# Query and key weights of two kinds of attention layer: kept on chip, or loaded block by block

## The chip, the cores and the metric

The kernel runs on one core of one Trainium2 chip. The metric is the device time of one execution in microseconds (us). The kernel before was run three times for its time, and once more with the hardware profiler, from which come the trace and the profile page.

## The reference

Four attention layers are applied in turn to an input of 2048 rows and 640 columns in bf16, each as `x = x + attention(layernorm(x))`. There are 32 heads of 20 columns. Layers 0 and 2 (kind A) let a row see itself and the 255 rows ahead of it; layers 1 and 3 (kind B) let each row see all rows. Layers of one kind share their weights.

```python
def _A_ref(x, wqkv, wo):
    B, S, D = x.shape
    H = 32; Dh = D // H; W = 256
    qkv = (lambda x, *d: x.transpose(*d))((x @ wqkv).reshape(B, S, 3, H, Dh), 2, 0, 3, 1, 4)
    q, k, v = qkv[0], qkv[1], qkv[2]
    scores = jnp.einsum("bhqd,bhkd->bhqk", q, k) * (Dh ** -0.5)
    idx = jnp.arange(S)
    mask = (idx[:, None] - idx[None, :] >= 0) & (idx[:, None] - idx[None, :] < W)
    scores = jnp.where(mask[None, None], scores, -1e9)
    p = _softmax(scores, axis=-1)
    o = jnp.einsum("bhqk,bhkd->bhqd", p, v)
    return (lambda x, *d: x.transpose(*d))(o, 0, 2, 1, 3).reshape(B, S, D) @ wo
...
x = x + _A_ref(_layernorm(x, axis=-1), A_wqkv, A_wo)
x = x + _B_ref(_layernorm(x, axis=-1), B_wqkv, B_wo)
x = x + _A_ref(_layernorm(x, axis=-1), A_wqkv, A_wo)
x = x + _B_ref(_layernorm(x, axis=-1), B_wqkv, B_wo)
```

`_B_ref` is the same without the mask. The layer norm has no scale and no offset.

## The kernel before, in words

**Stages and tiles.** The rows are cut into 4 chunks of 512 (`C`). For each layer and chunk the kernel normalises the rows and transposes them into a tile `xnT` of 128 x 5 x 512 (`t_ln`, L410), projects queries, keys and values from it, forms the attention, and adds the product with the output weights to `x_sb`, which stays on chip (`t_out`, L565). Heads go in 8 groups of four, one head to each 32 rows or columns of the PE array. A unit (`Unit`, L694) is one layer, chunk and group, for layers 1 and 3 also a part of the keys. All units stand in one list (L752 to L768), in which windowed units of layer A are woven between full ones of layer B.

**The main loop** (L1371) writes the program tile by tile. For each tile t it takes two or three score blocks of the current unit, has PE form them in PSUM (L1416), and ACT take the exponentials into a tile `pt` (L1442). Two or three tiles later PE multiplies `pt` by the values (L1475). For windowed units GpSimd (POOL in the profile) sets the masked part of `pt` to zero with selects (L1515), and VectorE (DVE) multiplies by mask tiles (L1526).

**Background work.** All else is a list of generators, `todo` and `tails`, sorted by the unit that needs them, of which `pump` (L265) advances some between two tiles by a credit. `require` (L299) is the way out: when a unit begins and something it needs is missing, tasks are advanced with no tiles in between. Each engine works its instructions in the order written; Tile adds the semaphores. `keep_clock` (L671) and `unread` (L659) add idle matmuls of `masks` by `ident` where PE has little to do.

**Query and key weights before.** In the first chunk of layer 0 (`t_qk_first`, L530) each group's 80 columns are copied from `raw`, which holds the weights of kind A, into a padded tile with 20 of every 32 columns used (`get_w`, L355 to L362: a memset on GpSimd and a copy on DVE, 16 times). Everywhere else (`t_block`, L545) a task projects 128 dense columns, one of 5 blocks of the queries or keys, and stores the result to DRAM (L554, on GpSimd's queue). For each of these 15 x 10 = 150 tasks `get_w` loads the block of weights from DRAM on GpSimd's queue (L353, 160 KB) into one of 8 buffers of the pool `wqkp`. `take_w` (L364) starts the loads of up to two blocks ahead, and holds the task until four tiles after its load was issued (`wtick`).

**Other queues.** SP's queue (SyncE) first loads the input and the weights of the start (L128 to L138), then the output weights (L150), and, as they come due, each unit's queries, keys and values (`load_unit`, L781). GpSimd's queue also carries the stores of projections and values and, in `t_ln`, the square root of each chunk's norm (L421, L424).

**Normed rows.** The pool `xtp` has five `xnT` buffers; `room` (L320) lets a task go on only while fewer than `cap` are in use, and `used` (L329) gives one back when all its 9 to 12 projections are written.

**DVE's share of the exponentials.** In layers 1 and 3 a part of the score blocks goes in pairs to DVE, which forms the exponential by arithmetic (`side_fixed`, L975, `chain`, L997). `side_start` (L911) sets up its scratch tiles for layer 3 from three `xnT` buffers that are no longer in use; `side_early` (L924) does so for layer 1 in another tile.

Of the kernel before, what the change touches and what calls it, by code (L numbers as in the profile page):

```python
# [9 lines left out]
BF16 = mybir.dt.bfloat16  # L10
# [8 lines left out]
P = 128  # L19
S = 2048  # L20
D = 640
# [38 lines left out]
def kernel(  # L60
# [14 lines left out]
    def pool(name, bufs, space=None):  # L75
        kw = {"space": space} if space else {}
        return ctx.enter_context(tc.tile_pool(name=name, bufs=bufs, **kw))

    big = pool("big", 1)
    wqkp = pool("wqkp", 8)  # L80
    kvp = pool("kvp", 3)
    vap = pool("vap", 10)
    xtp = pool("xtp", 5)
    onp = pool("onp", 2)
    ptp = pool("ptp", 6)
    stp = pool("stp", 4)
# [12 lines left out]


    x_sb = big.tile([P, NT, D], BF16, name="x_sb", tag="x_sb")
    raw = big.tile([P, KD, 2 * D], BF16, name="raw", tag="early_late")
    wv_sb = [big.tile([P, KD, D], BF16, name=f"wv{w}", tag=f"wv{w}") for w in range(2)]
    wop = big.tile([P, G, D], BF16, name="wop", tag="wop")
    ident = big.tile([P, P], BF16, name="ident", tag="ident")
# [209 lines left out]
            nc.tensor.matmul(out_[r], lhsT=lhsT[:, r], rhs=rhs, start=start, stop=stop)  # L315

    live = Counter()
    cap = {"qa": QA, "ka": KA, "va": 10, "xnT": 5, "kt": 3, "vt": 3, "qt": 4, "ln": 1, "w": 4, "vs": 2}

    def room(*tags):  # L320
        while any(live[t] + tags.count(t) > cap[t] for t in tags):
# [4 lines left out]

    users = {}

    def used(l, c):  # L329
        users[l, c] -= 1  # L330
        if users[l, c] == 0:
            live["xnT"] -= 1

    def evac(out_, in_):
        if state["act"]:
# [4 lines left out]


    wtiles = {}
    worder = {(l, n): [] for l in range(4) for n in range(2)}

    wtick = {}

    def get_w(l, n, c, i):

        t = wqkp.tile([P, KD, P], BF16, name="wqk", tag="wqk")
        wtick[l, n, c, i] = state["tick"] + 4  # L350
        if l or c:
            a = n * D + i * P
            nc.gpsimd.dma_start(out=t[:], in_=wq_view[l % 2][:, :, a : a + P])  # L353
            return t
        tv = t[:].rearrange("p c (j m) -> p c j m", j=4)  # L355
# [5 lines left out]
        wtick[l, n, c, i] = 0  # L361
        return t  # L362

    def take_w(l, n, c, i):  # L364
        key, order = (l, n, c, i), worder[l, n]
        if key not in wtiles:
            wtiles[key] = get_w(*key)
        while state["tick"] < wtick[key]:
            yield ("wait", 1)
        at = order.index(key)  # L370
        order.pop(at)
        wt = wtiles.pop(key)
        for e in order[at : at + 2]:
            if e not in wtiles and sum(o in wtiles for o in order) < 2 and len(wtiles) < 4:
                wtiles[e] = get_w(*e)
        return wt

    staging = []

# [30 lines left out]
    def t_ln(l, c):  # L410
        while ("x", l, c) not in ready:
            yield ("wait", 1)
        yield from room("xnT", "ln")
        for n in (1, 0):
            order = worder[l, n]
            if order and not any(e in wtiles for e in order):
                wtiles[order[0]] = get_w(*order[0])
# [12 lines left out]
        xt = xtp.tile([P, KD, C], BF16, name="xnT", tag="xnT")  # L430

        def normed(i):
            state["lag"] += 0.5
            xn = xnp.tile([P, D], BF16, name="xn", tag="xn")
            nc.vector.tensor_scalar(
                out=xn[:], in0=x_sb[:, 4 * c + i, :],
                scalar1=rstd[:, i : i + 1], scalar2=nmr[:, i : i + 1],
                op0=ALU.mult, op1=ALU.add,
            )
# [24 lines left out]
        ready.add(("xnT", l, c))  # L464
# [65 lines left out]
    def t_qk_first(l, c, g):  # L530
        while ("xnT", l, c) not in ready:
            yield ("wait", 1)
        yield from room("qa", "ka", "w", "w")
        wt = yield from take_w(l, 0, c, g)
        q = qa_free.popleft()
        yield from project(wt, xnT[l, c], lambda: q[:])
        wt = yield from take_w(l, 1, c, g)
        k = ka_free.popleft()
        yield from project(wt, xnT[l, c], lambda: k[:])
        live["w"] -= 2  # L540
        qa[c, g], ka[c, g] = q, k
        used(l, c)
        ready.add(("qk", l, c, g))

    def t_block(l, n, c, b):  # L545

        while ("xnT", l, c) not in ready:
            yield ("wait", 1)
        yield from room("w")
        wt = yield from take_w(l, n, c, b)  # L550
        yield from project(wt, xnT[l, c], staged)
        rows = slice(b * P, (b + 1) * P)
        dst = k_d[l][rows, c * C : (c + 1) * C] if n else q_d[l][c, rows, :]
        nc.gpsimd.dma_start(out=dst, in_=staging.pop())  # L554
        live["w"] -= 1
        used(l, c)
        ready.add(("qk"[n], l, c, b))

# [67 lines left out]
    def push_layer(l, c):  # L626
# [10 lines left out]
        if c or l:  # L637
            for b in range(KD):
                g = b * P // 80
                for n in (1, 0):  # L640
                    worder[l, n].append((l, n, c, b))
                    first = index[l, c, g, PARTS[l][0] if l % 2 and c == 0 else None]
                    first = need[g] if n else first
                    push(("qk"[n], l, c, b), t_block(l, n, c, b), first, 1.1)
            return
        for g in range(G):
            for n in (0, 1):
                worder[l, n].append((l, n, c, g))
# [261 lines left out]

    def side_start():  # L911

        assert live["xnT"] <= 2 and not side["chain"] and side["half"] is None
        tl = [xtp.tile([P, KD, C], BF16, name="xnT", tag="xnT") for _ in range(3)]
        live["xnT"] += 3
        f = [v[:, 0:4, :].rearrange("p a b -> p (a b)").bitcast(F32) for v in tl]
        side["xi"].clear()
        side["out"].clear()
        outs = [ka_all[:, KA - 6 + 2 * n : KA - 4 + 2 * n, :] for n in range(3)]
        outs += [qa_all[:, 2 * n : 2 * n + 2, :] for n in range(2)]  # L920
        side_tiles(f[0:2], f[2].bitcast(F16)[:, 0 : 2 * C], outs)
        side["late"] = True

    def side_early():  # L924
# [311 lines left out]
    def first_ln():  # L1236

        users[0, 0] = 9
        live["xnT"] += 1
        xt = xtp.tile([P, KD, C], BF16, name="xnT", tag="xnT")  # L1240

        def warm(count):
            for n in range(count):
# [42 lines left out]
        warm(3)  # L1286
        nc.vector.tensor_copy(out=xt[:, :, P : 2 * P], in_=trs[1])
        for n in (1, 0):
            wtiles[0, n, 0, 0] = get_w(0, n, 0, 0)
# [6 lines left out]
    with tc.manual_schedule():  # L1296
# [74 lines left out]
        while ended is None or t < ended + 8:  # L1371
# [3 lines left out]
            if flow:  # L1375
                if not side["early"] and state["unit"] >= index[1, 1, 0, None]:
                    side_early()
                if (
                    not side["late"] and state["unit"] >= index[3, 0, 4, PARTS[3][0]]
                    and live["xnT"] <= 1 and not live["qa"] and not live["ka"]  # L1380
                ):
                    side_start()
                if state["unit"] >= final:
# [191 lines left out]
```

## Time and profile before

| | us |
|---|---|
| three runs: median (lowest, highest) | 2168.42 (2165.64, 2171.8) |
| the profiled execution, its own time | 2167.19 |
| span of its trace | 2165.5 |
| ACT busy in it | 2086.1 |
| PE busy | 1924.8 |
| DVE busy | 1488.7 |
| POOL busy | 485.9 |

The span is the time from the first to the last instruction on the core, and lies 1.7 us below that execution's own time. A busy engine is one that executes; its waits are listed as idle time, with what ended them. PEld is PE's loading of weights, which lies beside its matmuls. Traffic with DRAM is 99.52 MB read and 27.79 MB written.

### The profile page before, as it was taken

The page shows a single profiled execution, that of the slowest core. Times are in us where ns is not written, and L with a number is a line of the kernel's source. Part 1 is how long each engine was busy: PE and PEld are TensorE (multiplying, and loading weights), DVE is VectorE, ACT ScalarE, POOL GpSimd, SP SyncE. Part 2 cuts the span into 40 slices and gives each one's busy share as a digit, 9 for nine tenths or more (in the row PEclk, how much of TensorE's full clock was granted, in tenths as well). Part 3 has the DMA queues.
Part 4 walks back from the last instruction along what each step waited for, and adds up shares of the span by engine and source line. Part 5 has one row for each costly group of instructions (what it writes and reads, how often), then busy time and mean ns, then how long its engine had stood idle before and what let it go on. Part 6 is the DMA issues. An engine that isn't in the chain of part 4 may idle for free. (4 is left out here: it accounts for less than half of the span.)

```text
span 2165.5 us, 73279 instructions
## 1 busy us (share of the span) xinstructions
PE 1924.8 (89%) x31759; PEld 754.6 (35%) x31759; DVE 1488.7 (69%) x2625; ACT 2086.1 (96%) x1717; POOL 485.9 (22%) x953
## 2 busy tenths in 40 slices
PE   8999999988889898888988989888898898888898
PEld 4444443433333333333333433332332222222222
DVE  5656665426666776776767733676779887888896
ACT  7889899999999999999999999989999999999997
POOL 6665546110122113410053112511000000000000
PEclk9999999999999999999999999999999999999999
DMA  6223233322211323112241133112121111111100
GB/s 204 76 84 107 75 92 101 81 80 64 79 45 27 84 61 90 41 41 61 56 112 33 37 86 99 39 42 77 53 60 44 35 36 42 32 33 39 42 30 17
DMA packets 88418, 137.29 MB, mean 63 GB/s; under 512 B 20766, under 2 KB 63486, under 8 KB 88094
## 3 DMA queue, kind: packets, MB, share of 16 engines
q1 hardware_dynamic: 68878, 79.43, 13.9%
q0 software_dynamic: 19216, 53.17, 8.3%
q8 instruction: 249, 4.08, 0.8%
q14 instruction: 75, 0.61, 0.1%
HBM read 99.52 MB, written 27.79 MB: 59 GB/s over the span
## 5 line engine op out<-in xcount | busy, mean ns | idle before, releaser
L1442 ACT ACTIVATE pt<-ps 128x1536 bf16<-128x1536 f32 (+2 forms) x1641 | 2051.7, 1406 | 46.4 <-PE ps L1416 35.5
L1416 PE MATMUL ps<-qt,kt 32*128 32x512 bf16 x3914 | 544.6, 383 | 59.8 <-ACT pt L1442 52.5
L315 PE MATMUL ps<-masks,ident 128*32 128x512 bf16 x5652 | 505.6, 384 | 96.6 <-ACT pt L1442 47.5
L1475 PE MATMUL ps<-pt,vt 128*21 128x512 bf16 x3774 | 375.9, 386 | 1.8 <-issue 1.0
L1416 PEld LDWEIGHTS <-kt 32*128 32x128 bf16 x3914 | 154.7, 91 | 460.2 <-issue 440.4
L315 PEld LDWEIGHTS <-ident 128*32 128x32 bf16 x5652 | 180.3, 94 | 278.9 <-issue 253.5
L1515 POOL TENSOR_SCALAR_AFFINE_SELECT pt<-pt 128x256 bf16<-128x256 bf16 (+2 forms) x506 | 217.1, 451 | 187.6 <-ACT pt L1442 175.3
L315 PE MATMUL ps<-xnT,wqk 128*32 128x512 bf16 x3320 | 225.2, 381 | 11.9 <-DMA wqk<-in_B_wqkv_dram 2.1
L339 DVE CAST st<-ps 128x512 bf16<-128x512 f32 x134 | 92.5, 690 | 143.9 <-PE ps L315 143.6
L1475 PEld LDWEIGHTS <-vt 128*21 128x21 bf16 x3774 | 93.4, 89 | 260.1 <-issue 256.3
L989 DVE TENSOR_SCALAR xnT<-ps 128x512 int32<-128x512 f32 x210 | 144.1, 687 | 34.6 <-PE ps L971 27.5
L315 PE MATMUL ps<-wop,on 128*32 128x320 bf16 x3712 | 160.5, 300 | 5.7 <-DVE x_sb L587 3.9
L1526 DVE TENSOR_TENSOR pt<-pt,masks 128x256 bf16<-128x256 bf16 (+3 forms) x268 | 113.4, 438 | 46.5 <-ACT pt L1442 44.3
L315 PEld LDWEIGHTS <-on 128*32 128x32 bf16 x5760 | 122.3, 95 | 63.7 <-issue 29.8
L1416 PE MATMUL ps<-qa,ka 32*128 32x384 bf16 (+2 forms) x1408 | 118.0, 276 | 22.5 <-ACT pt L1442 19.1
L587 DVE TENSOR_TENSOR x_sb<-x_sb,ps 128x320 bf16<-128x320 bf16 x120 | 58.2, 485 | 101.6 <-PE ps L315 101.1
L1185 DVE TENSOR_TENSOR on<-on,ps 128x512 bf16<-128x512 bf16 x128 | 86.4, 684 | 59.2 <-PE ps L315 57.0
L315 PE MATMUL ps<-wv,xnT 128*32 128x320 bf16 x2560 | 116.0, 301 | 9.0 <-DVE vs L339 2.0
L315 PEld LDWEIGHTS <-wqk 128*32 128x32 bf16 x3320 | 83.2, 96 | 96.0 <-issue 38.1
L989 DVE TENSOR_SCALAR raw_o<-ps 128x512 int32<-128x512 f32 x112 | 76.8, 686 | 47.3 <-PE ps L1416 46.8
L890 DVE CAST on<-ps 128x512 bf16<-128x512 f32 x112 | 76.7, 685 | 37.9 <-PE ps L1475 30.7
L554 POOL DMA_DIRECT2D k_d<-st x75 | 42.5, 567 | 225.7 <-DVE st L339 213.0
(99 smaller groups left out, 1797.9 us busy)
## 6 DMA issues: line engine op xcount, KB each, us to landing
vt<-v_d SPq DMA_DIRECT2D x48, 336.0 KB
kt<-k_d SPq DMA_DIRECT2D x192, 80.0 KB
wqk<-in_B_wqkv_dram POOLq DMA_DIRECT2D x80, 160.0 KB, 3.5
wqk<-in_A_wqkv_dram POOLq DMA_DIRECT2D x70, 160.0 KB, 3.6
k_d<-st POOLq DMA_DIRECT2D x75, 128.0 KB, 2.5
q_d<-st POOLq DMA_DIRECT2D x75, 128.0 KB, 2.3
qt<-q_d SPq DMA_DIRECT2D x384, 20.0 KB
v_d<-vs POOLq DMA_DIRECT2D x16, 336.0 KB, 3.0
```

The lines of the kernel that those rows point to most:

```text
L315: nc.tensor.matmul(out_[r], lhsT=lhsT[:, r], rhs=rhs, start=start, stop=stop)
L339: nc.vector.tensor_copy(out=out_, in_=in_)
L554: nc.gpsimd.dma_start(out=dst, in_=staging.pop())
L587: nc.vector.tensor_tensor(out=xv, in0=had, in1=yp, op=ALU.add)
L890: nc.vector.tensor_copy(out=oT, in_=op)
L989: nc.vector.tensor_scalar(out=xi.bitcast(I32)[:, i * C : (i + 1) * C], in0=z, scalar1=SCALE * LOG2E * FIX, scalar2=127.5 * FIX, op0=ALU.mu ...
L1185: nc.vector.tensor_tensor(out=oT, in0=oT, in1=zb, op=ALU.mult)
L1416: nc.tensor.matmul(sp[:, i, col * P : (col + qn) * P], lhsT=u.k(kc, j), rhs=u.q(j, q0, qn), start=True, stop=True,)
L1442: nc.scalar.activation(out=pt[:, i:k, b0 * P :], in_=sp[:, i:k, b0 * P :], func=ACT.Exp, scale=SCALE,)
L1475: nc.tensor.matmul(op[32 * j : 32 * j + VW, q0 * P : (q0 + qn) * P], lhsT=u.v(kc, j), rhs=pg[:, i, col * P : (col + qn) * P], start=(first ...
L1515: nc.gpsimd.affine_select(out=v, in_=v, compare_op=ALU.is_gt if later else ALU.is_ge, fill=0.0, base=0, pattern=[[0, k - i], [-1 if later ...
L1526: nc.vector.tensor_tensor(out=pt_[:, i:k, cols], in0=pt_[:, i:k, cols], in1=mv_, op=ALU.mult)
```

## The change

- The pools `wqkp` and `xtp` go. One tile `xt_all` has two slots for normed rows in the place of five buffers, handed out by `take_xt` and given back by `used`.
- One tile `spare`, as large as three of the former buffers, holds `raw` (kind A's query and key weights) and behind it the last 256 columns of kind B's. A tile `wqk` of 1024 columns is first the eight padded buffers of the first chunk and then holds the first 1024 columns of kind B's.
- After the last padded projection two loads on SP's queue bring kind B's weights. Tasks of layers 1 and 3 are not started before these loads are written.
- `t_block` takes its weights from these tiles (`block_w`). There are no loads by block, no order of loads and no holding for four tiles; `t_ln` starts no load.
- `side_start` takes its scratch from `spare`, over `raw`, at a point where layer 2's projections are all written, and no longer looks at how many `xnT` buffers are in use.

```diff
-    wqkp = pool("wqkp", 8)
-    xtp = pool("xtp", 5)
...
-    raw = big.tile([P, KD, 2 * D], BF16, name="raw", tag="early_late")
+    xt_all = big.tile([P, 2, KD, C], BF16, name="xnT", tag="xnT")
+    spare = big.tile([P, 3 * KD * C], BF16, name="spare", tag="spare")
+    raw = spare[:, 0 : KD * 2 * D].rearrange("p (c f) -> p c f", c=KD)
+    wqk_rest = spare[:, KD * 2 * D :].rearrange("p (c f) -> p c f", c=KD)
+    wqk = big.tile([P, KD, 8 * P], BF16, name="wqk", tag="wqk")
...
-    cap = {"qa": QA, "ka": KA, "va": 10, "xnT": 5, "kt": 3, "vt": 3, "qt": 4, "ln": 1, "w": 4, "vs": 2}
+    cap = {"qa": QA, "ka": KA, "va": 10, "xnT": 2, "kt": 3, "vt": 3, "qt": 4, "ln": 1, "w": 4, "vs": 2}
...
-        wtick[l, n, c, i] = state["tick"] + 4
-        if l or c:
-            a = n * D + i * P
-            nc.gpsimd.dma_start(out=t[:], in_=wq_view[l % 2][:, :, a : a + P])
-            return t
...
-        while state["tick"] < wtick[key]:
-            yield ("wait", 1)
...
+    def block_w(l, n, b):
+
+        a = n * D + b * P
+        if l % 2 == 0:
+            return raw[:, :, a : a + P]
+        if a < 8 * P:
+            return wqk[:, :, a : a + P]
+        return wqk_rest[:, :, a - 8 * P : a - 7 * P]
...
+        if g == G - 1:
+            nc.sync.dma_start(out=wqk[:], in_=wq_view[1][:, :, 0 : 8 * P])
+            nc.sync.dma_start(out=wqk_rest, in_=wq_view[1][:, :, 8 * P : 2 * D])
+            ready.add("weights")
...
-        yield from room("w")
-        wt = yield from take_w(l, n, c, b)
+        while l % 2 and "weights" not in ready:
+            yield ("wait", 1)
+        wt = block_w(l, n, b)
...
-        tl = [xtp.tile([P, KD, C], BF16, name="xnT", tag="xnT") for _ in range(3)]
-        live["xnT"] += 3
-        f = [v[:, 0:4, :].rearrange("p a b -> p (a b)").bitcast(F32) for v in tl]
+        f = [spare[:, n * 4 * C : (n + 1) * 4 * C].bitcast(F32) for n in range(2)]
...
-                    and live["xnT"] <= 1 and not live["qa"] and not live["ka"]
+                    and not live["qa"] and not live["ka"]
```

More of the change, by code (lines that the diff above doesn't have):

```diff
@@ L327, with take_xt @@
     users = {}
+    xt_free = deque(range(2))
+    xt_n = {}
+    def take_xt(l, c):
+        xt_n[l, c] = xt_free.popleft()
+        return xt_all[:, xt_n[l, c]]
     def used(l, c):
@@ L332, in used @@
             live["xnT"] -= 1
+            xt_free.append(xt_n.pop((l, c)))
     def evac(out_, in_):
@@ L342, with get_w @@
     wtiles = {}
[L343 to L349, printed above, removed]
-        wtick[l, n, c, i] = state["tick"] + 4
-        if l or c:
-            a = n * D + i * P
-            nc.gpsimd.dma_start(out=t[:], in_=wq_view[l % 2][:, :, a : a + P])
-            return t
-        tv = t[:].rearrange("p c (j m) -> p c j m", j=4)
+    worder = {(0, n): [] for n in range(2)}
+    padded = [0]
+    def get_w(n, i):
+        a = padded[0] % 8 * P
+        padded[0] += 1
+        t = wqk[:, :, a : a + P]
+        tv = t.rearrange("p c (j m) -> p c j m", j=4)
         nc.gpsimd.memset(tv[:, :, :, DH:32], 0.0)
@@ L360, in get_w, with take_w @@
         )
-        wtick[l, n, c, i] = 0
         return t
-    def take_w(l, n, c, i):
-        key, order = (l, n, c, i), worder[l, n]
+    def take_w(n, i):
+        key, order = (n, i), worder[0, n]
         if key not in wtiles:
             wtiles[key] = get_w(*key)
-        while state["tick"] < wtick[key]:
-            yield ("wait", 1)
         at = order.index(key)
@@ L413, in t_ln @@
         yield from room("xnT", "ln")
[L414 to L417, printed above, removed]
         users[l, c] = 9 if (l, c) == (0, 0) else (11, 12, 11, 11)[l]
@@ L429, in t_ln @@
         )
-        xt = xtp.tile([P, KD, C], BF16, name="xnT", tag="xnT")
+        xt = take_xt(l, c)
         def normed(i):
@@ L533, in t_qk_first @@
         yield from room("qa", "ka", "w", "w")
-        wt = yield from take_w(l, 0, c, g)
+        wt = take_w(0, g)
         q = qa_free.popleft()
         yield from project(wt, xnT[l, c], lambda: q[:])
-        wt = yield from take_w(l, 1, c, g)
+        wt = take_w(1, g)
         k = ka_free.popleft()
@@ L554, in t_block @@
         nc.gpsimd.dma_start(out=dst, in_=staging.pop())
-        live["w"] -= 1
         used(l, c)
@@ L640, in push_layer @@
                 for n in (1, 0):
-                    worder[l, n].append((l, n, c, b))
                     first = index[l, c, g, PARTS[l][0] if l % 2 and c == 0 else None]
@@ L647, in push_layer @@
             for n in (0, 1):
-                worder[l, n].append((l, n, c, g))
+                worder[l, n].append((n, g))
             push(("qk", l, c, g), t_qk_first(l, c, g), need[g], 2.2)
@@ L911, in side_start @@
     def side_start():
-        assert live["xnT"] <= 2 and not side["chain"] and side["half"] is None
-        tl = [xtp.tile([P, KD, C], BF16, name="xnT", tag="xnT") for _ in range(3)]
-        live["xnT"] += 3
-        f = [v[:, 0:4, :].rearrange("p a b -> p (a b)").bitcast(F32) for v in tl]
+        assert not side["chain"] and side["half"] is None
+        assert ("k", 2, NC - 1, KD - 1) in ready and ("q", 2, NC - 1, KD - 1) in ready
+        f = [spare[:, n * 4 * C : (n + 1) * 4 * C].bitcast(F32) for n in range(2)]
         side["xi"].clear()
@@ L920, in side_start @@
         outs += [qa_all[:, 2 * n : 2 * n + 2, :] for n in range(2)]
-        side_tiles(f[0:2], f[2].bitcast(F16)[:, 0 : 2 * C], outs)
+        side_tiles(f[0:2], spare[:, 8 * C : 10 * C].bitcast(F16), outs)
         side["late"] = True
@@ L1239, in first_ln @@
         live["xnT"] += 1
-        xt = xtp.tile([P, KD, C], BF16, name="xnT", tag="xnT")
+        xt = take_xt(0, 0)
         def warm(count):
@@ L1288, in first_ln @@
         for n in (1, 0):
-            wtiles[0, n, 0, 0] = get_w(0, n, 0, 0)
+            wtiles[n, 0] = get_w(n, 0)
         nc.vector.tensor_copy(out=xt[:, :, 2 * P : 3 * P], in_=trs[2])
```

## The prediction

> **What bounds the kernel now.** I read the head of the profile page first, for the engine that has no slack, and then the view by stretches, for where its slack lies. The stretches are cut where the kinds of work change (the columns after the length are the busy time of PE, PE's weight loads, DVE, ACT and POOL, each with its instructions, then the granted clock, the DMA share and GB/s).
>
> ```profile
> span 2165.5 us, 73279 instructions
> PE 1924.8 (89%) x31759; PEld 754.6 (35%) x31759; DVE 1488.7 (69%) x2625; ACT 2086.1 (96%) x1717; POOL 485.9 (22%) x953
> ...
> 0.00:433.00 433.00, 394.56 (x8075) 185.02 (x8079) 252.46 (x587) 386.10 (x397) 235.16 (x494) 0.99 0.37 102
> 433.00:1407.00 974.00, 860.25 (x14487) 349.75 (x14479) 616.71 (x1190) 965.08 (x772) 234.81 (x435) 1.00 0.24 63
> 1407.00:1516.00 109.00, 93.56 (x1455) 37.00 (x1453) 78.41 (x123) 99.89 (x80) 15.96 (x24) 1.00 0.22 59
> 1516.00:2111.00 595.00, 531.30 (x7181) 166.81 (x7181) 506.42 (x672) 591.56 (x441) 0.00 (x0) 1.00 0.14 40
> ```
>
> ACT sets the time: it is idle for only 2165.5 - 2086.1 = 79.4 us, and by length less busy time 46.9 of these lie before 433 us, 8.9 up to 1407, 9.1 up to 1516 and 3.4 up to 2111, which leaves 11.1 for the tail. So a change that leaves ACT's instructions alone can win only what it takes out of these gaps, and the question is which gaps hang on the weight loads. I went through ACT's gaps of 0.3 us and more in the order of time and looked, for each, at what PE and POOL did just before. After 1516 none can hang on them: POOL has no work left.
>
> The loads by group (times | busy us, mean ns of one | idle before them), the matmuls that read them, and one row of the DMA part (size and median us to landing):
>
> ```profile
> L353 POOL DMA_DIRECT2D wqk<-in_B_wqkv_dram x80 | 69.7, 873 | 2.1 <-issue 1.5 <-PE ps L315 0.7
> L353 POOL DMA_DIRECT2D wqk<-in_A_wqkv_dram x70 | 60.9, 872 | 1.8 <-PE ps L1416 1.1 <-issue 0.7
> L315 PE MATMUL ps<-xnT,wqk 128*32 128x512 bf16 x3320 | 225.2, 381 | 11.9 <-DMA wqk<-in_B_wqkv_dram 2.1 <-DVE on L1185 1.4 <-ACT xnT L336 1.3
> ...
> wqk<-in_B_wqkv_dram POOLq DMA_DIRECT2D x80, 160.0 KB, 3.5
> ```
>
> The 150 issues cost POOL 69.7 + 60.9 = 130.6 us, but POOL is not the bound; and PE stood idle before the matmuls that use these weights for 11.9 us in all, few of them for a load. The change is therefore not worth 130 us but a few.
>
> **The change, part by part.**
>
> *Loads that PE waited for go.* Three places in the order of time, each with PE's wait and the ACT gap behind it (in brackets: idle before, and what ended it):
>
> ```profile
> 270.65 1.26 PE L315 MATMUL ps<-xnT,wqk 128*32 128x512 bf16 x20 [0.96 <-DMA wqk<-in_A_wqkv_dram]
> 272.56 1.45 ACT L1442 ACTIVATE pt<-ps 128x1536 bf16<-128x1536 f32 x1 [0.94 <-issue]
> 1246.09 1.26 PE L315 MATMUL ps<-xnT,wqk 128*32 128x512 bf16 x20 [1.13 <-DMA wqk<-in_B_wqkv_dram]
> 1247.78 1.45 ACT L1442 ACTIVATE pt<-ps 128x1536 bf16<-128x1536 f32 x1 [1.33 <-PE ps L1416]
> 1463.87 1.26 PE L315 MATMUL ps<-xnT,wqk 128*32 128x512 bf16 x20 [0.95 <-DMA wqk<-in_B_wqkv_dram]
> 1465.58 1.02 ACT L1442 ACTIVATE pt<-ps 128x1024 bf16<-128x1024 f32 x1 [0.77 <-PE ps L1416]
> ```
>
> Of each pair the smaller number is what can go: 0.94 + 1.13 + 0.77 = 2.84 us.
>
> *POOL issues that stood ahead of masks go.* POOL works in order, so a mask (L1515) behind two weight issues comes late, and PE's values product waits for it:
>
> ```profile
> 233.36 0.92 POOL L353 DMA_DIRECT2D wqk<-in_B_wqkv_dram  x1
> 235.59 0.86 POOL L353 DMA_DIRECT2D wqk<-in_B_wqkv_dram  x1
> 237.08 0.52 PE L1475 MATMUL ps<-pt,va 128*21 128x256 bf16 x5 [1.75 <-POOL pt L1515]
> 238.01 1.45 ACT L1442 ACTIVATE pt<-ps 128x1536 bf16<-128x1536 f32 x1 [2.21 <-POOL pt L1515]
> ...
> 1123.40 1.74 POOL L353 DMA_DIRECT2D wqk<-in_B_wqkv_dram  x2
> 1125.63 0.64 PE L1475 MATMUL ps<-pt,va 128*21 128x256 bf16 x6 [0.99 <-POOL pt L1515]
> 1127.13 1.45 ACT L1442 ACTIVATE pt<-ps 128x1536 bf16<-128x1536 f32 x1 [1.15 <-PE ps L1416]
> ```
>
> Here 0.92 + 0.86 = 1.78 us of issues cover PE's 1.75, and 1.74 cover its 0.99: 2.74 us go. A third place is less plain. Two issues precede seven masks, and a normalise on DVE beside those masks took 1.72 us where its line's median is 442 ns:
>
> ```profile
> 314.32 1.73 POOL L353 DMA_DIRECT2D wqk<-in_B_wqkv_dram  x2
> 316.06 3.01 POOL L1515 TENSOR_SCALAR_AFFINE_SELECT pt<-pt 128x256 bf16<-128x256 bf16 x7
> 316.72 1.72 DVE L435 TENSOR_SCALAR xn<-x_sb,rstd,nmr 128x640 bf16<-128x640 bf16 x1
> 319.62 2.54 ACT L1442 ACTIVATE pt<-ps 128x1024 bf16<-128x1024 f32 x2 [1.38 <-PE ps L1416]
> ...
> L435 DVE TENSOR_SCALAR xn<-x_sb,rstd,nmr x60: 428/442/1715, 48.3 to 1440.5; 128x640 bf16<-128x640 bf16 x60
> ```
>
> Without the issues the masks run earlier, and may or may not still meet a normalise: between 0 and 1.38, I take half, 0.69. [...]
>
> *Waits that PE no longer has.* In the compiled order PE's instructions that carry a wait fall from 4361 to 4226, as each load had one. At most the 11.9 us of idle time before these matmuls lie behind that. Of them 0.96 + 1.13 + 0.95 = 3.0 are counted above, and the next causes that the row names are DVE and ACT. So I take 0 for the rest and keep 11.9 - 3.0 = 8.9 as the other end; a loss has no reason here, since the matmuls and their order stay.
>
> *ACT's own work.* In the compiled order ACT has 1641 exponentials as before, but three more of 1536 columns, one more of 512 and four fewer of 1024, since DVE takes 104 late pairs of blocks instead of 105:
>
> ```profile
> L1442 ACT ACTIVATE pt<-ps 128x1536 bf16<-128x1536 f32 x1280 | 1766.9, 1524 | 37.1 <-PE ps L1416 27.0 <-POOL pt L1515 3.4 <-issue 1.7
> L1442 ACT ACTIVATE pt<-ps 128x1024 bf16<-128x1024 f32 x280 | 299.3, 1072 | 9.2 <-PE ps L1416 8.4
> L1442 ACT ACTIVATE pt<-ps 128x512 bf16<-128x512 f32 x24 | 14.4, 620 | 0.0
> ```
>
> Busy time per instruction is 1766.9/1280 = 1.380, 299.3/280 = 1.069 and 14.4/24 = 0.600: 3 x 1.380 + 0.600 - 4 x 1.069 = +0.46 us.
>
> *What is added.* Two loads on SP's queue, 1.31 and 0.33 MB, behind the last padded projection of the first chunk, which is where SP would otherwise stand idle. That projection ends near 49 us; queued behind it is the load of the next unit:
>
> ```profile
> 4.62 2.07 SPq L135 DMA_DIRECT2D wv<-in_A_wqkv_dram  x1
> ...
> 39.59 2.28 SPq L150 DMA_DIRECT2D wop<-in_A_wo_dram  x4
> ...
> 47.70 1.26 PE L315 MATMUL ps<-xnT,wqk 128*32 128x512 bf16 x20 [0.36 <-DVE on L1185]
> ...
> 62.56 0.30 SPq L792 DMA_DIRECT2D qa<-q_d  x1
> ...
> 41.90:62.50 20.60, 17.06 (x390) 7.94 (x383) 11.98 (x34) 15.98 (x26) 15.03 (x29) 1.00 0.53 120
> L353 POOL DMA_DIRECT2D wqk<-in_B_wqkv_dram x80: 852/867/999, 116.2 to 1482.9; - x80
> ```
>
> The 0.8 MB load held SP for 2.07 us, so two loads of twice that hold it until about 53, and the unit's load comes at 62.56: hidden. At the 120 GB/s of that stretch 1.64 MB take 14 us, landed by some 67; the first B block was loaded at 116.2, so nothing waits. If the cover were gone, those 14 us less the stretch's spare half would be the price, some 7 us.
>
> *Two normed-row slots instead of five.* A third chunk must wait until one of two is used up. In the compiled order ACT's list matches before for its first 159 instructions, has the same 1719 in all, and no block of projections comes more than eight tiles later (many come up to 20 earlier, as the four-tile wait after each load is gone). I cost it at nothing; the rivals price it. The side tiles' move into the old weights, and the padded copies (16 as before), change only addresses, and stay beside ACT's exponentials; were each padded copy slower by half, DVE, at 252 of 433 us, still has the room.
>
> *Sum.* 2.84 + 2.74 + 0.69 - 0.46 = 5.81 us off. A stall that goes lets the next wait show: in the row of these matmuls above PE waits 1.4 us for DVE's L1185 and 1.3 for ACT's copies as well. This has no row of its own; I take off a sixth for it, which leaves 4.9 us. The profiled execution took 2167.2 us (its span and 1.7 around it), which gives 2162.3; from the median of 2168.4 it would be 2163.5. I forecast 2163.0, between these.
>
> **The rivals.**
>
> *More comes off: 2158.* PE's clock was granted at half for a while (0.50 in the last row; the first is the whole slice), just after a lull in which PE had little to do and POOL was full:
>
> ```profile
> 54.10:108.30 54.20, 49.34 (x1137) 24.85 (x1134) 33.21 (x90) 44.28 (x61) 35.05 (x76) 0.94 0.27 76
> ...
> 86.00:88.00 2.00, 0.67 (x7) 0.20 (x7) 1.66 (x5) 2.00 (x3) 1.99 (x5) 1.00 0.57 168
> ...
> 90.00:92.00 2.00, 2.00 (x56) 0.70 (x56) 1.52 (x5) 1.77 (x3) 1.83 (x4) 0.50 0.18 39
> ```
>
> A slice of 54.2 us at 0.94 has lost 3.3 us of PE, or 6.5 us at half, in a place where PE is full (2.00 of 2.00). With POOL eased the lull may not come: 5.8 + 3.3 = 9.1 us off, and 2167.2 - 9.1 = 2158. For it: POOL was at 1.99 of 2.00. Against: in the lull ACT was busy for the whole 2.00 us, so PE waited for ACT and not for POOL. [...]
>
> *Nothing arrives: 2167 to 2170.* Each freed gap is met by a DVE or PE wait; then the 0.46 us more of ACT and the spread of the three runs (2165.6 to 2171.8) remain. For it: PE is at 394.56 of 433 in the stage with most gaps.
>
> *Slower: 2185.* With two slots a chunk's norm can come so late that a unit reaches its first tile before its projections exist; they then run with no exponentials beside them. Such a place costs four normalises (4 x 0.44 us), two blocks (2 x 1.26) and a store and a load to landing, each by the nearest row 3.5: 1.8 + 2.5 + 7.0 = 11.3 us. One gives 2162.3 + 11.3 = 2173.6, still within 0.3%; it decides from the second, 2162.3 + 22.6 = 2185. For it: each of the fifteen later chunks passes through these slots, and PE and DVE have little room to catch up before 433 us. Against: the compiled order shows no such run of projections, and ACT's list hardly changes.
>
> **How the numbers follow.** A measurement tells 0.3%, 6.5 us, from no change; faster by that is below 2161.9. Forecast (2162 to 2167): 0.52; more: 0.31; nothing: 0.07; slower: 0.10, with the single late place in the 0.07. So faster 0.31, same 0.59, slower 0.10. The range reaches from 2155 (the 2158 and a third of the 8.9 us) to 2170.
>
> **What would show it.** POOL busy near 485.9 - 130.6 = 355 us; no PE wait for a weight load; the six gaps gone and ACT's idle near 74 us with its busy time within 1 us; a clock of 1.00 from 54 to 108 us would speak for the first rival. Wrong would be: ACT idle unchanged, or a long row of projections with ACT waiting.

## The result: 2165.3 us, a little faster, and the profile after

The kernel after took 2165.28 us (median of 20 runs, 2160.35 to 2166.91), the kernel before beside it 2167.70 us (20 runs, 2163.58 to 2174.15). The ratio is 0.9983, with a 95% interval of 0.9976 to 0.9991: faster, by less than the 0.3% that the prediction took for a difference. Two later series gave 0.9975 [0.9964, 0.9985] and 0.9980 [0.9971, 0.9989]. The profiled execution took 2161.81 us, 5.4 less than that of before.

The head of the page of after, one row of its DMA part, and the four stretches of the prediction (same columns):

```profile
span 2160.1 us, 73113 instructions
PE 1925.8 (89%) x31774; PEld 755.2 (35%) x31775; DVE 1484.4 (69%) x2619; ACT 2085.4 (97%) x1717; POOL 360.2 (17%) x803
HBM read 76.58 MB, written 27.79 MB: 48 GB/s over the span
```

```profile
0.00:433.00 433.00, 397.01 (x8121) 186.42 (x8125) 255.85 (x588) 387.89 (x399) 179.93 (x429) 0.99 0.28 82
433.00:1407.00 974.00, 861.62 (x14542) 351.36 (x14535) 618.33 (x1194) 967.47 (x774) 171.20 (x358) 1.00 0.18 50
1407.00:1516.00 109.00, 93.20 (x1427) 35.97 (x1426) 75.83 (x119) 99.51 (x79) 9.05 (x16) 0.98 0.18 49
1516.00:2111.00 595.00, 533.27 (x7173) 167.12 (x7170) 502.77 (x668) 592.52 (x441) 0.00 (x0) 1.00 0.14 40
```

POOL lost 125.7 us of work and DRAM 23 MB of reading, and the time moved by 5.4 us: ACT's idle time went from 79.4 to 2160.1 - 2085.4 = 74.7 us. Its busy time is 0.7 us less. ACT has 45.1 us of idle time before 433 (46.9) and 6.5 up to 1407 (8.9), but 9.5 up to 1516 (9.1). Beside this last figure stands a clock of 0.98 in that row, a piece of half clock that comes up again below.

The two new loads on SP's queue cost nothing. They hold the queue for 0.39 and 0.53 us, and the next unit's load comes at 61.70 (62.56 before):

```profile
50.01 0.39 SPq L554 DMA_DIRECT2D wqk<-in_B_wqkv_dram  x1
50.45 0.53 SPq L555 DMA_DIRECT2D spare<-in_B_wqkv_dram  x1
61.70 0.32 SPq L804 DMA_DIRECT2D qa<-q_d  x1
```

Now the matmuls that read these weights, by group. In after the group is two, since the weights lie in two tiles:

```profile
L317 PE MATMUL ps<-xnT,spare 128*32 128x512 bf16 x1720 | 118.2, 381 | 5.5 <-DVE on L1196 1.8
L317 PE MATMUL ps<-xnT,wqk 128*32 128x512 bf16 x1600 | 108.1, 381 | 6.7 <-DVE xnT L1301 1.3
```

No weight load is among the causes any more (3.0 us before), and yet PE's idle time before these matmuls is 5.5 + 6.7 = 12.2 us, where it was 11.9. Other waits stand there now. The place near 279 us shows one in full, engine by engine (start, duration, and in brackets the idle time before and what ended it):

```profile
273.98 1.83 POOL L1526 TENSOR_SCALAR_AFFINE_SELECT pt<-pt 128x128 bf16<-128x128 bf16 x5
274.16 1.79 DVE L1537 TENSOR_TENSOR pt<-pt,masks 128x256 bf16<-128x256 bf16 x1
275.87 1.27 DVE L1196 TENSOR_TENSOR on<-on,ps 128x512 bf16<-128x512 bf16 x2
276.60 1.53 PE L317 MATMUL ps<-wv,xnT 128*32 128x320 bf16 x20 [1.48 <-DVE on L1196]
279.24 1.45 ACT L1453 ACTIVATE pt<-ps 128x1536 bf16<-128x1536 f32 x1 [2.30 <-issue]
```

Read it from below: ACT waits 2.30 us (its row names no releaser), because PE came late, because PE waited 1.48 us for two products of DVE, which stood behind a mask multiply that took 1.79 us; an operation of that shape took 0.28 us at 272.32. It lay beside five masks of POOL that end at 275.81, 0.14 us before it. This gap is not in before. About half of its length is the clock's: from 276.64 to 280.06 this profile has a granted clock of 0.50, and the twenty matmuls of the PE row took 1.53 us. In the two later profiles of after PE waits 1.49 and 1.47 us at this place, the same matmuls take 0.86 us, and ACT waits 1.22 and 1.21. A second gap that grew (0.80 before, at 164.84) has the same releaser:

```profile
162.97 1.26 PE L317 MATMUL ps<-xnT,spare 128*32 128x512 bf16 x20 [1.40 <-DVE on L1196]
164.93 2.36 ACT L1453 ACTIVATE pt<-ps 128x1536 bf16<-128x1536 f32 x2 [1.55 <-PE ps L1427]
```

It is 1.55 or 1.56 us in all three profiles of after. So two things happened: the gaps that hung on loads went, and the order without the four-tile wait brought gaps of its own. The experiments part the two.

### The profile page after: what moved, and what is told of

It is laid out like the page before. It is cut to its first block, busy times and chain, and to the rows that moved or that the text cites. A ratio compares the mean times of both kernels' runs of the same rounds, so it can differ in the third digit from the quotient of the medians.

```text
span 2160.1 us, 73113 instructions
## 1 busy us (share of the span) xinstructions
PE 1925.8 (89%) x31774; PEld 755.2 (35%) x31775; DVE 1484.4 (69%) x2619; ACT 2085.4 (97%) x1717; POOL 360.2 (17%) x803
## 5 line engine op out<-in xcount | busy, mean ns | idle before, releaser
L1526 POOL TENSOR_SCALAR_AFFINE_SELECT pt<-pt 128x256 bf16<-128x256 bf16 (+2 forms) x506 | 217.9, 452 | 199.4 <-ACT pt L1453 186.5
L1000 DVE TENSOR_SCALAR spare<-ps 128x512 int32<-128x512 f32 x208 | 142.8, 687 | 29.5 <-PE ps L982 23.1
L317 PE MATMUL ps<-xnT,spare 128*32 128x512 bf16 x1720 | 118.2, 381 | 5.5 <-DVE on L1196 1.8
L317 PE MATMUL ps<-xnT,wqk 128*32 128x512 bf16 x1600 | 108.1, 381 | 6.7 <-DVE xnT L1301 1.3
```

The source lines that it names most:

```text
L1000: nc.vector.tensor_scalar(out=xi.bitcast(I32)[:, i * C : (i + 1) * C], in0=z, scalar1=SCALE * LOG2E * FIX, scalar2=127.5 * FIX, op0=ALU.mu ...
L1526: nc.gpsimd.affine_select(out=v, in_=v, compare_op=ALU.is_gt if later else ALU.is_ge, fill=0.0, base=0, pattern=[[0, k - i], [-1 if later ...
```

## The experiments

The theory after the result: the change takes two kinds of stall away, PE's waits for loads and POOL's issues ahead of masks, worth more than the 6.3 us that the prediction found for them; and it gives a part back through the order, since without the four-tile wait other work meets on PE, DVE and POOL. The rivals: only PE's waits matter; the 23 MB of traffic matter; the order is worth nothing and the difference is the clock's.

The granted clock differs between runs of one kernel (the 64 runs of before that list it have 0.990 to 0.999), and each run lists its mean. Over the 182 runs of these kernels that list a clock, straight lines with a common slope give 1.2 us for each 0.001 of mean clock; single runs scatter about their lines by 1.4 us (standard deviation). The last column is each kernel's time on its line at 0.998, so that a chance difference in clock is not read as a kernel's. It can't judge a change that is meant to raise the clock, as the last experiment is.

| kernel | median us (runs) | ratio to before, 95% | at clock 0.998 |
|---|---|---|---|
| before | 2167.7 to 2169.3 in four series | | 2167.2 (the three later series) |
| after, three series | 2165.28 (20), 2163.58 (7), 2165.16 (12) | 0.9983, 0.9975, 0.9980 | 2162.2, 2161.2, 2162.3 |
| paced | 2161.20 (6), 2160.90 (6) | 0.9961 [0.9948, 0.9974], 0.9962 [0.9950, 0.9974] | 2159.5, 2159.4 |
| paced_issue | 2165.23 (12) | 0.9987 [0.9974, 1.0001] | 2164.0 |
| paced_sync | 2158.84 (5) | 0.9953 [0.9937, 0.9969] | 2158.6 |
| fill | 2158.61 (5), 2159.97 (6) | 0.9954 [0.9939, 0.9970], 0.9954 [0.9941, 0.9968] | 2159.6, 2159.3 |
| issue_150 | 2168.54 (11) | 0.9994 [0.9985, 1.0004] | 2165.6 |
| issue_300 | 2181.00 (5) | 1.0057 [1.0044, 1.0070] | 2178.8 |
| hold_8 | 2169.24 (11) | 1.0000 [0.9992, 1.0009] | 2166.9 |
| before_sync | 2172.33 (12) | 1.0014 [1.0003, 1.0024] | 2169.3 |

**The kernel after again**, beside the next three runs (a_again) and later beside its paced form (after_b):

> The changed kernel itself, beside the others on the same chip. Theory (six gaps go, and some is given back where PE, POOL and DVE meet at new times): ratio to before 0.9975 to 0.999. Rival (the order of the tasks decides, not the loads): the same here. It also shows how the granted clock of before and after compare over several runs: if more stretches at half clock take back a part of the gain, after's mean clock is 0.001 or more below before's.

> The kernel after again, on one chip with its paced form: ratio to before 0.9975 to 0.9985 if the earlier runs hold; 0.996, as its paced form, if the difference between the two was the chip's.

The three series agree within 1.7 us of median, and the kernel after stays 0.2% under before.

**The order put back (paced).** The weights stay on chip, and the four-tile wait is kept as bookkeeping without a load, so that the order on ACT, DVE and PE is that of before, and on POOL too but for the loads. The two slots for normed rows stay as in after.

```diff
+    def begin(key):
+        begun[key] = state["tick"] + 4
+
+    def paced(l, n, c, b):
...
+        while state["tick"] < begun[key]:
+            yield ("wait", 1)
...
+        yield from room("w")
+        yield from paced(l, n, c, b)
```

> Resident weights with before's pacing: tasks are held for four tiles as if their block were still loaded, so every engine has before's order of instructions to the letter, without the 150 loads. Theory: all six gaps go and ACT's extra 0.46 us does not come, so 5 to 6 us off, ratio 0.9972 to 0.998, at least as good as after. Rival 1 (the shifted order made the gain): ratio 0.9995 to 1.0005. Rival 2 (less traffic on the DMA queues made it): as after, 0.998 to 0.999.

> The kernel after with the four-tile pacing of before, again, on one chip with the next two. If the order is worth what the first run of it gave, the ratio to before is 0.996 and it is 2 to 3 us under the kernel after.

Twice 0.996, which is more than the first expectation's range (0.9972 to 0.998), and on one chip 2160.90 against 2165.16 us for after. At equal clock the order of after costs some 2.5 us, give or take 1 (an estimate from the scatter of 1.4 us over 39 and 12 runs). As paced has before's order, its ACT rows can be laid beside the gaps of before one for one. These are the stretches in its second profile that cover all places named in the prediction, and one more:

```profile
236.93 2.42 ACT L1484 ACTIVATE pt<-ps 128x1536 bf16<-128x1536 f32 x2 [0.59 <-POOL pt L1557]
...
263.54 9.27 ACT L1484 ACTIVATE pt<-ps 128x1536 bf16<-128x1536 f32 x8
...
305.39 13.19 ACT L1484 ACTIVATE pt<-ps 128x1536 bf16<-128x1536 f32 x11
...
409.47 2.36 ACT L1484 ACTIVATE pt<-ps 128x1536 bf16<-128x1536 f32 x2 [0.55 <-PE ps L1458]
...
1120.56 6.62 ACT L1484 ACTIVATE pt<-ps 128x1536 bf16<-128x1536 f32 x5
...
1237.09 8.14 ACT L1484 ACTIVATE pt<-ps 128x1536 bf16<-128x1536 f32 x6
...
1453.99 7.32 ACT L1484 ACTIVATE pt<-ps 128x1536 bf16<-128x1536 f32 x6 [0.30 <-PE ps L1458]
```

A row of eleven exponentials in 13.19 us without a bracket is an engine that hardly waited. Where before waited 2.21, 0.94, 1.38, 1.15, 1.33 and 0.77 us, paced waits 0.59 and then next to nothing: some 7.1 us are gone. The seventh, at 409.47, was 1.92 us in before and had not been counted, as the trace names no cause for PE's pause in front of it:

```profile
413.44 0.39 PE L1475 MATMUL ps<-pt,vt 128*21 128x512 bf16 x2 [0.98 <-issue]
...
414.54 2.36 ACT L1442 ACTIVATE pt<-ps 128x1536 bf16<-128x1536 f32 x2 [1.92 <-PE ps L1416]
```

It is 0.55 us in both kernels that have no loads by block (another 1.37). Together that is some 8.5 us, beside 7.7 between paced and before at equal clock. What holds PE there is open, and so is whether it goes with the loads. Pauses of PE without a cause in the trace stand in few profiles: before has another of 1.45 us at 51.61, and the first profile of paced, without loads, has one of 1.17 at 52.24 which its second has not. It isn't POOL: before_sync below, with its loads on SP's queue, has a pause of 1.20 us at 420.32, the same place in its order. The same two groups of matmuls in paced:

```profile
L317 PE MATMUL ps<-xnT,spare 128*32 128x512 bf16 x1720 | 117.9, 381 | 4.8 <-ACT xnT L347 1.4 <-DVE on L1227 1.1 <-DVE st L350 0.9
L317 PE MATMUL ps<-xnT,wqk 128*32 128x512 bf16 x1600 | 107.3, 381 | 4.9 <-DVE rts L1206 1.3 <-DVE vs L350 1.2 <-ACT vs L347 0.7
```

9.7 us here, 12.2 in after: in after the place of the loads was taken by waits for DVE, in paced it was not. The gap of 2.30 us isn't in paced either: between the same products DVE copies out a projection of queries or keys there, of values in after, and the mask multiply takes 0.28 us.

**POOL's issues put back, without their use (issue_150, issue_300, paced_issue).** Each task of a block issues its old load on POOL's queue, into a scratch in DRAM that nobody reads; issue_300 issues two. PE waits for none of them.

```diff
+    away = [dram.tile([P, KD, P], BF16, name=f"away{n}", tag=f"away{n}") for n in range(8)]
...
+        nc.gpsimd.dma_start(out=away[aways[0] % 8][:], in_=wq_view[l % 2][:, :, a : a + P])
```

> After with 150 block loads still issued by POOL, into a scratch tensor in DRAM that nobody reads: POOL's 130 us and the traffic are back, PE's waits for the loads are not. Theory: the places where POOL came late with masks are back (2.7 to 3.4 us lost against after) and the 2.8 us of load waits stay away: ratio 0.9985 to 1.0. Rival 1 (order): as after, 0.998 to 0.9985. Rival 2 (traffic): 1.0 or above.

> The same with two such loads in each place: POOL's issue time is doubled to some 260 us. Theory: each late mask comes later still by up to 0.87 us a load, 3 to 8 us slower than with 150: ratio 1.0 to 1.004. Rival 1 (order): as after. Rival 2 (traffic): slower by as much as the step from none to 150.

> Before's order on every engine, resident weights, and POOL still issues the 150 loads (into DRAM, read by nobody). Only PE's waits for loads are gone. Theory: 2 to 3.5 us under before (ratio 0.9984 to 0.999), and 4 to 6 us over the same kernel without the issues. Rival (the order of after is what made the version with 150 issues slow): within 2 us of the kernel without the issues, 0.996 to 0.997.

On after, 150 issues cost some 3.5 us at equal clock, and 150 more cost 13.2: not in proportion, and above the expected 3 to 8, as the groups of issue_300 show. Two issues in a row take 1.3 to 1.4 us each (1377 ns in the row below, 1307 for the 140 loads of kind A), and its masks took 252.6 us (217.9 in after).

```profile
L568 POOL DMA_DIRECT2D away<-in_B_wqkv_dram x160 | 148.8, 1377 | 0.8 <-issue 0.8
L1532 POOL TENSOR_SCALAR_AFFINE_SELECT pt<-pt 128x256 bf16<-128x256 bf16 (+2 forms) x506 | 252.6, 672 | 161.1 <-ACT pt L1459 150.0 <-issue 9.2 <-DVE pt L1543 0.8
```

In paced_issue the order on PE, DVE and ACT is that of before. It is 3.1 us under before at equal clock, though the interval of its ratio reaches 1.0001, and paced_issue less paced is what its issues cost (4.6 us; 4.0 by the medians). One issue takes as long as in before (71.3 us for 80 of them, 69.7 there). But they do not stand where before has them: a task issues when it runs, and not four tiles or more ahead, which in the compiled order is 12 POOL instructions later on average. So the 3.1 and the 4.6 don't part before's own gaps; a run further down does that. Two places in the trace of paced_issue, a mask behind an issue and a mask beside DVE:

```profile
233.86 0.81 POOL L596 DMA_DIRECT2D away<-in_B_wqkv_dram  x1
236.82 0.52 PE L1522 MATMUL ps<-pt,va 128*21 128x256 bf16 x5 [1.02 <-POOL pt L1562]
237.76 1.45 ACT L1489 ACTIVATE pt<-ps 128x1536 bf16<-128x1536 f32 x1 [1.48 <-POOL pt L1562]
...
275.44 0.82 POOL L596 DMA_DIRECT2D away<-in_A_wqkv_dram  x1
276.11 1.86 POOL L1562 TENSOR_SCALAR_AFFINE_SELECT pt<-pt 128x128 bf16<-128x128 bf16 x5
276.32 2.00 DVE L1573 TENSOR_TENSOR pt<-pt,masks 128x256 bf16<-128x256 bf16 x1
279.23 2.37 ACT L1489 ACTIVATE pt<-ps 128x1536 bf16<-128x1536 f32 x2 [0.72 <-POOL pt L1562]
```

The first is the place of the prediction's 1.75, with one issue in front now and 1.48 us on ACT in the place of 2.21. In the second the issue holds the masks back by 0.82 us, so that five of them stand in a row, and they meet the mask multiply: 2.00 us in the place of 0.28. At these two places issues cost by the masks that they delay, and by what those then meet.

**The traffic alone (paced_sync).** The same 150 copies, on SP's queue.

```diff
-        nc.gpsimd.dma_start(out=away[aways[0] % 8][:], in_=wq_view[l % 2][:, :, a : a + P])
+        nc.sync.dma_start(out=away[aways[0] % 8][:], in_=wq_view[l % 2][:, :, a : a + P])
```

> The same, but the 150 loads go out on SP's queue: the traffic is back, POOL's issues are not. Theory (POOL's time and its meetings with DVE make the second half of the gain): as without any loads, 0.996 to 0.9972. Rival (traffic): as with the issues on POOL, 0.9984 to 0.999. SP's queue takes 150 issues more, and where a unit's loads stand behind them it could lose 1 to 2 us.

It lies under the expected range, not over it: at equal clock 0.8 us under paced, no more than five runs can tell. The rival of the traffic falls: 25 MB more to read and as much to write cost nothing that shows. (These copies are written to DRAM, where before's loads were written on chip.)

**The loads themselves on SP's queue (before_sync).** One word of before is changed, PE's waits for the weights stay, and the order on PE, DVE and ACT is the same.

```diff
-            nc.gpsimd.dma_start(out=t[:], in_=wq_view[l % 2][:, :, a : a + P])
+            nc.sync.dma_start(out=t[:], in_=wq_view[l % 2][:, :, a : a + P])
```

> The kernel before, with its 150 block loads issued on SP's queue in the place of POOL's; order on PE, DVE and ACT as before, and PE still has the weights' waits. Theory that POOL's issues and their meetings with DVE are the larger half: about 4 us under before (2164), with PE's waits for weight loads still in the trace (about 3 us in all). Rival, that PE's waits are the larger half: within 1.5 us of before. If SP's queue is held by a load that waits for its buffer, units' loads come late and it is slower than before.

The expected gain did not come; the last sentence of the expectation did, with the roles turned: it is the weights that are late, not the units' loads.

```profile
165.15 0.33 SPq L793 DMA_DIRECT2D ka<-k_d  x1
165.58 0.39 SPq L353 DMA_DIRECT2D wqk<-in_B_wqkv_dram  x1
166.07 0.53 SPq L353 DMA_DIRECT2D wqk<-in_A_wqkv_dram  x1
166.69 0.47 SPq L353 DMA_DIRECT2D wqk<-in_B_wqkv_dram  x1
...
168.28 1.27 PE L315 MATMUL ps<-xnT,wqk 128*32 128x512 bf16 x20 [3.17 <-DMA wqk<-in_B_wqkv_dram]
170.18 3.45 ACT L1442 ACTIVATE pt<-ps 128x1024 bf16<-128x1024 f32 x3 [3.48 <-PE ps L1416]
```

Three weight loads stand in the queue behind the unit's loads of queries and keys (sixteen of them from 157.16 to 165.15), PE waits 3.17 us for one, and ACT 3.48. In all, PE's idle time before these matmuls is 17.7 us, 5.8 more than in before:

```profile
L315 PE MATMUL ps<-xnT,wqk 128*32 128x512 bf16 x3320 | 226.3, 382 | 17.7 <-DMA wqk<-in_B_wqkv_dram 5.6 <-DMA wqk<-in_A_wqkv_dram 2.9 <-DVE on L1185 1.5
```

The time doesn't weigh POOL's issues, as was meant, but the trace does, place by place. The three gaps of the prediction that hung on masks, 2.21, 1.38 and 1.15 us at 238.01, 319.62 and 1127.13 in before, lie in these rows:

```profile
242.42 4.89 ACT L1442 ACTIVATE pt<-ps 128x1536 bf16<-128x1536 f32 x4 [0.59 <-POOL pt L1515]
318.63 9.41 ACT L1442 ACTIVATE pt<-ps 128x1536 bf16<-128x1536 f32 x8
1100.02 59.45 ACT L1442 ACTIVATE pt<-ps 128x1536 bf16<-128x1536 f32 x46
```

0.59 and twice nothing are left, as in paced, although all 150 blocks are still loaded: 1.62 + 1.38 + 1.15 = 4.15 us of before's gaps were POOL's issues, by one profile of each kernel. So the rival that only PE's waits matter falls too. New gaps like the 3.48 outweigh that (ACT is idle 2169.1 - 2085.9 = 83.2 us, 3.8 more than in before), and the kernel is 2.2 us slower at equal clock. Another queue isn't the remedy where residence is.

**A longer hold (hold_8).** Paced with 8 in the place of 4.

```diff
-        begun[key] = state["tick"] + 4
+        begun[key] = state["tick"] + 8
```

> Tasks held for eight tiles instead of four (none in after), no loads: another order of the same work, 104 to 105 pairs on DVE. If moving tasks by a few tiles changes the time by itself through where masks and DVE operations meet, as after against the paced kernel suggests (2 to 3 us), this one lies 0 to 5 us off the paced kernel, either way: 0.995 to 0.9985. Rival (only the one pair that ACT took over, 0.5 us, separates after and paced): within 1 us of the paced kernel.

All weights are on chip, no load by block is issued, and nothing is won: 7.4 us are lost to paced at equal clock, more than the 0 to 5 expected, by the order with its few extra operations (11 more on DVE, 100 more matmuls on PE of 31759). Its trace has many gaps of 0.4 to 0.8 us that paced has not, and one of 3.78 us, in a stretch of 15 us (1490 to 1505) with a clock of 0.77:

```profile
1499.82 1.45 ACT L1484 ACTIVATE pt<-ps 128x1536 bf16<-128x1536 f32 x1 [3.78 <-PE ps L1458]
```

**Idle matmuls for the lull near 88 us (fill).** Paced with some forty idle matmuls more (31803 in the profile, 31759 in that of paced), to try the prediction's first rival by itself.

```diff
-            if state["early"] and mfree[b][0] > state["tick"]:
-                break
...
-            state["least"] = (1.76 if state["unit"] >= woven else 1.0) * n_b / 3
+            state["least"] = (1.76 if state["unit"] >= woven else 2.5) * n_b / 3
```

> Before's order, resident weights, and ten groups of idle matmuls more, nine of them where PE has next to nothing to do at 84 to 90 us (all other engines unchanged). Theory that the half clock after that lull is bought by the lull: the stretch at half clock at 89 to 96 us goes, the mean clock rises by 0.0015, and 1 to 3 us come off against the kernel without them: ratio 0.995 to 0.996. [...]

> The paced form with forty idle matmuls more, again, on one chip with it. If the lull near 88 us costs a half clock that these matmuls ward off: 2 to 3 us under the paced form, with a mean clock of 0.998 or more and no slice under 0.98. If the first run of it only met a chip with a better clock: within 1 us of the paced form.

In both profiles of fill the clock stays at 1.00 from 84 to 96 us. But so it does in the second profile of paced, without the matmuls, while after, with the same lull, had 0.50 from 88.91 to 95.74. The same stretch in after, paced (second profile) and fill:

```profile
84.00:88.00 4.00, 2.30 (x44) 1.03 (x36) 3.27 (x10) 3.88 (x5) 3.49 (x8) 1.00 0.22 76
88.00:92.00 4.00, 3.60 (x78) 1.23 (x75) 3.03 (x11) 3.76 (x4) 3.31 (x8) 0.61 0.14 35
```

```profile
84.00:88.00 4.00, 2.30 (x44) 1.03 (x36) 3.28 (x10) 3.88 (x5) 3.47 (x8) 1.00 0.24 78
88.00:92.00 4.00, 3.15 (x90) 1.43 (x86) 3.26 (x11) 4.00 (x4) 3.31 (x8) 1.00 0.17 35
```

```profile
84.00:88.00 4.00, 3.26 (x60) 1.30 (x52) 2.84 (x9) 3.88 (x5) 3.50 (x8) 1.00 0.28 91
88.00:92.00 4.00, 3.81 (x106) 1.79 (x106) 3.58 (x12) 4.00 (x4) 3.31 (x8) 1.00 0.17 31
```

Still, the second profile of paced is the exception: in the other eleven profiles of kernels without these matmuls, its first among them, the clock from 82 to 100 us is 0.72 to 0.91 (0.81 in before and in after). Both profiles of fill lose clock later, 0.96 and 0.91 from 200 to 240 us, where paced has 0.91 and 0.96. On one chip fill took 2159.97 us and paced 2160.90 (means 2159.5 and 2161.0, over 6 runs each), and over all its 11 runs fill lists a mean clock of 0.998 where the 12 of paced list 0.9965. At equal clock they are alike, as they must be if the clock is all that the matmuls change. So the runs speak for a small gain by the clock (1.5 us between the means on one chip, with an interval of 0.3 to 2.8, where 2 to 3 were expected). Two profiles don't prove that it comes from the lull at 88 us.

## Why the prediction was right, and which terms were off

**The sum.** 4.9 us off were forecast from the profiled execution. The profiled pair differs by 5.4, the medians by 2.4 to 4.7, and at equal clock it is 5.1. The forecast of 2163.0 lies 2.3 us under the first median and within the range. The mechanism was right, but the sum came out by luck in part: some 8 us of stalls went and the order took some 2.5 back, and the prediction had both too small. (A sixth of 5.81 is 0.97, so its own sum gives 4.84 and not 4.9.)

**"Loads that PE waited for go", 2.84.** Right: in paced ACT's gaps at the three places fell from 0.94, 1.33 and 0.77 us to next to nothing. (Two of the three, 1.33 and 0.77, also went in before_sync, where the loads come by another queue.)

**"POOL issues that stood ahead of masks go", 2.74 and 0.69.** Too small: 4.15 us at these three places in before_sync and in paced. The third place was taken at half of 1.38. In paced it went altogether (the 13.19 us row), though five masks are still made there in a row, from 313.88 to 315.98, and a normalise still runs beside them:

```profile
314.22 0.64 DVE L471 TENSOR_SCALAR xn<-x_sb,rstd,nmr 128x640 bf16<-128x640 bf16 x1
```

It took 0.64 us where before's took 1.72. In after the normalises there took 0.64 and 0.48 us beside five masks, and ACT waits 0.74 us for another reason: PE waits for nothing there, but a projection of 1.26 us (at 320.69) now stands between two groups of scores.

```profile
322.62 3.71 ACT L1453 ACTIVATE pt<-ps 128x1536 bf16<-128x1536 f32 x3 [0.74 <-PE ps L1427]
```

So masks that stay in a row do not keep such a gap by themselves: beside them a normalise took 1.72 us in before and 0.64 in paced, and a mask multiply 1.79 in after and 2.00 in paced_issue, where one took 0.28 at other times. What decides it is open. The gap at 414.54 wasn't counted, since no load and no late mask stands in front of it; that it belongs to the loads isn't shown.

**"Waits that PE no longer has", 0, other end 8.9.** Nearly right: beyond the counted waits 1.37 us went, at 414.54, and these perhaps by the run. What went is far from the other end, since DVE and ACT's copies end most of that idle time in paced too.

**"ACT's own work", 0.46, and "a sixth" of the gains for the next wait.** This is the step that failed in size, and it was priced on the wrong engine. ACT's busy time is 2086.1 us in before, 2085.4 to 2085.7 in the three profiles of after and 2086.0 and 2085.4 in those of paced, so a term of 0.46 can't be told from the spread. What the changed order costs, some 2.5 us between after and paced, is new idle time of ACT. Its two largest pieces, some 1.2 us at 279.24 and 0.75 at 164.93, hang on PE's waits for DVE (1.48 and 1.40 in the rows above), and the 0.74 on a projection in the way. The prediction had seen that blocks come up to 20 tiles earlier "as the four-tile wait after each load is gone", and costed that move at nothing. The sixth (0.9) covered part of it by chance.

**"What is added" and "Two normed-row slots", 0.** Right: the loads held SP's queue for 0.92 us, not 4, and no unit came late. Two slots alone were not run, but paced has two slots and, compiled, the order of before on PE, ACT and DVE, so they held nothing up.

**The rivals.** *More comes off*: the slice from 54.1 to 108.3 us has 0.94 in after as before, with POOL eased from 35.05 to 28.10 us:

```profile
54.10:108.30 54.20, 48.96 (x1144) 24.71 (x1136) 32.98 (x91) 44.08 (x61) 28.10 (x67) 0.94 0.21 63
```

The objection held: the lull is not POOL's. In after PE's longest wait in it, 1.18 us at 86.92, ends with an exponential of ACT, as the 0.85 us at 87.12 did in before. The dip stands in eleven of twelve profiles, but not in every run of a kernel: paced has 0.94 in one profile and 1.00 in the other. *Nothing arrives* fell with POOL's and PE's gaps gone. *Slower* fell as there is no run of projections with ACT waiting; but hold_8 shows that a changed order can take back all that residence gives, by another mechanism than the slots.

**A version that is faster than both** came out of it: paced, at 0.9961 and 0.9962, is 7.1 and 8.4 us under before by the medians, where after is 2.4 to 4.7 under it.

## What to carry to other kernels

A removed load is worth the stalls that hang on it, and those are to be counted at the bounding engine's gaps, place by place: here 130 us of POOL's issues and PE's waits for 150 loads were worth 8 us, and 23 MB of traffic nothing that shows. When a load goes, look whether its wait also set the order of other work: keep that order first (a counter does), and change it in a step of its own. And when a load is moved to another engine's queue, look at what is in that queue already: in before_sync three weight loads stood behind sixteen loads of units on SP's queue, PE waited 3.17 us for one, and its idle time before these matmuls was 17.7 us, where it was 11.9 with the loads on POOL's queue.

## What the runs showed of the hardware

In the profiles of before and after the half clock came in pieces of 3.41 us or twice that. Leaving out the last microsecond of the span, before has one, 6.83 us from 89.41; after has one of 6.83 from 88.91 and two of 3.41, from 276.64 and from 1498.62. Not all places are the same in two runs of one kernel: from 54.1 to 108.3 us paced has 0.94 in one profile and 1.00 in the other. The last piece of after lies where before had a clock of 1.00:

```profile
1498.00:1503.00 5.00, 4.95 (x48) 1.14 (x51) 0.69 (x1) 4.77 (x5) 0.00 (x0) 0.66 0.15 36
```

(1 - 0.66) x 5 = 1.7 us are lost, which is 3.4 us at half. In after_b more is lost in one stretch: 0.91 from 54.1 to 108.3 us is 4.9 us, or 9.8 at half. By these lengths one piece of 3.4 us is worth up to 1.7 us of PE where PE is full (an estimate), beside 2.5 us for the order above: two kernels that differ by so little are best compared at the same mean clock, unless the change is one of the clock itself.

Beside masks that POOL made in a row an operation of DVE took longer at some places and not at others: a mask multiply, 0.28 us at 272.32 in after, took 1.79 and 1.78 us beside five masks in the profiles of after and after_b, and 2.00 in paced_issue. The normalise above took 0.64 us beside five masks in paced, where the median of its line is 0.44.
